# A pre-norm transformer layer on one core: more DMA transposes, zero tiles ahead of the first projection, and x of chunk 1 loaded ahead of the v weights

## The chip, the cores and the metric

One core of a Trainium2 chip runs the whole layer. The metric is the device time of one execution in microseconds (us); lower is better. Each time is printed beside the span of the trace (first to last instruction), and the time was the span plus 1.7 to 2.0 us, mostly 1.8, in every run of this case. In the profile's lines PE is TensorE (matrix products), DVE is VectorE, ACT is ScalarE, POOL is GpSimd and SP is SyncE, which issues most DMA transfers. The granted clock is the share of its full clock that TensorE was given; a stretch below it is called cold here. A zero tile is a matrix product of zeros whose result nobody uses.

Every set of runs was taken with runs of the kernel before on the same chip. A ratio compares a kernel's fast runs with the fast runs of the kernel before in the same rounds. It is therefore not quite the ratio of the medians quoted beside it. Below 1 is faster. Runs marked slow are left out of ratios.

## The reference, cut to what matters

```python
x = A_x                                            # 1 x 2048 x 512, bf16
h  = x + attention(layernorm(x), wqkv) @ wo        # 32 heads of 16; each position looks at
                                                   # 8 keys, 2 apart, itself and backwards
h2 = h + (relu_gate(layernorm(h) @ W_gate) * (layernorm(h) @ W_up)) @ W_down   # F = 1376
```

## The kernel before

The 2048 rows go in four chunks of 512, and a chunk in four blocks of 128 rows. Per chunk: layer norm, transposes, q/k/v projections on TensorE; products q times shifted k on VectorE (`pr`, 128x4096, 2.3 us each), sums over a head on TensorE; products of weights and v on VectorE (`mu`), whose eight terms are then added up; output projection; second norm; MLP. TensorE's work of one chunk covers the waits of another. The order of every instruction on every engine comes from a list of ranks, `RANK`, worked out beforehand from assumed durations. The parts that matter here:

```python
# setup: loads in the order of their queue
for j in range(BPC):                       # x of chunk 0, four blocks, two issuers
    (nc.scalar if j % 2 else nc.sync).dma_start(x_sm[:, j:j + 1, :], x_rows[:, j:j + 1, :])
for c, q in enumerate((nc.sync, nc.scalar, nc.sync)):          # q, k, v weights
    q.dma_start(w3_sb[c][:], w3_r[:, :, c * D:(c + 1) * D])
for tk in range(1, NCK):                                       # x of chunks 1, 2, 3
    nc.sync.dma_start(x_sm[:, tk * BPC:(tk + 1) * BPC, :], x_rows[:, tk * BPC:(tk + 1) * BPC, :])
# ... (cut: other weights)

# layer norm: a block is transposed by a DMA or on TensorE
if (ln, tk, j0) in DMAT:
    nc.sync.dma_start_transpose(out=dst.t[:, :, j * P:(j + 1) * P], in_=xn.t[:])
# ... else four nc.tensor.transpose and an eviction

# attention: the first of three halvings of the eight v products, 128x2048
if n == 4 and (tk, t) in DACC:
    nc.gpsimd.dma_start(mt.t[:, 0:4, :], mt.t[:, 4:8, :], accum_op=ALU.add)   # an accumulating DMA
# ... else one VectorE add

DACC = tuple((k, t) for k in range(3) for t in range(4))       # chunks 0 to 2, all four
DMAT = (("h",2,0),("h",2,2),("x",3,0),("x",3,2))               # x3 and the second norm of chunk 2
NWARM = 48                                                     # opening zero tiles on TensorE
```

The softmax here doesn't subtract the row's maximum and nothing guards it: scores larger than these inputs give would overflow.

Of the kernel before, what the change touches and what calls it, by code (L numbers as in the profile page):

```python
# [8 lines left out]
P = 128  # L9
# [3 lines left out]
ACT = mybir.ActivationFunctionType  # L13
# [4 lines left out]
RANK = [  # L18
    1, 3, 5, 2, 0, 4, 54, 6, 7, 30, 160, 197, 186, 250, 712, 8, 11, 10, 12, 14,
    17, 23, 27, 32, 20, 26, 31, 16, 18, 21, 24, 28, 33, 37, 9, 13, 15, 19, 22, 25,  # L20
    29, 34, 35, 65, 71, 68, 70, 73, 38, 60, 66, 56, 63, 69, 51, 61, 43, 55, 40, 50,
    45, 58, 83, 145, 79, 154, 76, 162, 74, 99, 80, 86, 96, 104, 110, 75, 67, 85, 89, 90,
    171, 179, 185, 114, 136, 123, 133, 128, 94, 113, 101, 108, 118, 148, 159, 183, 189, 193, 156, 170,
    199, 203, 205, 165, 176, 201, 204, 207, 142, 152, 181, 187, 192, 211, 218, 210, 215, 214, 222, 209,
    212, 227, 234, 221, 225, 228, 232, 226, 231, 239, 241, 246, 256, 249, 257, 261, 244, 259, 251, 260,
    264, 292, 321, 277, 317, 267, 313, 324, 333, 340, 280, 305, 270, 304, 301, 308, 303, 310, 315, 295,
    325, 307, 328, 285, 323, 319, 329, 335, 327, 344, 297, 341, 331, 346, 314, 339, 349, 350, 366, 343,
    358, 338, 365, 355, 372, 392, 334, 359, 348, 362, 397, 401, 421, 691, 717, 393, 407, 694, 718, 357,
    420, 701, 721, 363, 423, 699, 720, 39, 47, 44, 48, 36, 41, 42, 46, 49, 52, 62, 78, 64,
    77, 82, 57, 81, 59, 72, 84, 144, 191, 124, 188, 91, 178, 102, 182, 88, 164, 109, 169, 143,  # L30
    172, 117, 168, 147, 252, 139, 300, 87, 299, 151, 302, 195, 174, 224, 245, 229, 208, 238, 248, 253,
    258, 268, 273, 271, 284, 293, 296, 294, 290, 275, 283, 286, 287, 289, 298, 309, 345, 352, 318, 330,
    361, 367, 326, 337, 364, 368, 306, 316, 347, 351, 373, 378, 379, 386, 376, 382, 383, 395, 385, 389,
    391, 396, 390, 394, 398, 400, 402, 403, 406, 413, 408, 415, 419, 411, 417, 412, 418, 422, 431, 456,
    427, 454, 433, 460, 426, 452, 494, 439, 469, 441, 471, 434, 462, 436, 463, 500, 438, 466, 437, 465,
    479, 488, 464, 474, 503, 487, 496, 484, 491, 489, 498, 493, 501, 507, 450, 518, 458, 517, 506, 523,
    499, 520, 526, 447, 508, 444, 509, 524, 516, 536, 709, 726, 510, 530, 707, 725, 522, 538, 705, 723,
    533, 537, 703, 722, 98, 105, 92, 97, 93, 103, 53, 95, 112, 116, 126, 132, 125, 130, 146, 131,
    137, 129, 135, 150, 167, 216, 177, 217, 184, 220, 194, 223, 161, 240, 157, 237, 163, 242, 153, 213,
    173, 428, 175, 409, 202, 416, 219, 356, 236, 254, 265, 312, 274, 263, 288, 320, 322, 332, 336, 342,  # L40
    360, 353, 377, 375, 369, 374, 371, 384, 387, 381, 380, 430, 435, 453, 459, 414, 429, 446, 449, 424,
    432, 451, 457, 399, 425, 443, 448, 467, 473, 461, 468, 475, 482, 470, 478, 477, 480, 472, 476, 485,
    486, 481, 483, 490, 495, 519, 521, 511, 513, 528, 531, 497, 502, 543, 559, 540, 558, 549, 568, 548,
    565, 573, 560, 585, 567, 582, 575, 588, 544, 561, 594, 556, 578, 583, 593, 554, 576, 579, 590, 596,
    552, 570, 563, 580, 546, 564, 553, 574, 591, 616, 625, 572, 618, 599, 621, 608, 623, 631, 620, 630,
    587, 628, 633, 626, 642, 715, 731, 612, 639, 713, 729, 597, 635, 711, 727, 600, 640, 714, 730, 100,
    106, 115, 121, 111, 119, 107, 120, 122, 127, 140, 149, 155, 166, 134, 141, 138, 158, 247, 281, 180,
    255, 196, 269, 190, 266, 243, 279, 235, 278, 200, 272, 230, 276, 233, 541, 198, 505, 262, 550, 206,
    545, 291, 282, 311, 404, 370, 354, 388, 405, 410, 440, 442, 492, 445, 504, 529, 534, 527, 532, 455,
    525, 514, 515, 512, 542, 562, 581, 586, 535, 539, 555, 569, 551, 557, 566, 571, 547, 577, 584, 589,  # L50
    595, 603, 604, 611, 598, 607, 592, 601, 606, 609, 614, 615, 610, 613, 602, 605, 617, 619, 622, 624,
    636, 637, 641, 627, 634, 629, 632, 638, 646, 660, 650, 663, 647, 661, 644, 656, 675, 667, 677, 665,
    674, 673, 681, 670, 678, 684, 659, 671, 654, 668, 657, 669, 662, 672, 682, 651, 664, 652, 666, 643,
    655, 645, 658, 679, 683, 695, 648, 686, 680, 693, 649, 689, 697, 653, 688, 676, 690, 696, 685, 706,
    728, 736, 692, 700, 716, 732, 687, 702, 719, 734, 698, 704, 724, 735, 708, 710, 733, 737,
# [36 lines left out]
class Plan:  # L92
# [21 lines left out]
    GUIDE = ()  # L114

    def order(self):
        for kx, cx, ky, cy in self.GUIDE:
            xs = [o for o in self.ops if o.key and o.key[0].startswith(kx) and o.key[1] == cx]
            for o in self.ops:
                if o.key and o.key[0].startswith(ky) and o.key[1] == cy:  # L120
                    o.deps += xs
        waiting = list(self.ops)
        free = {}
        while waiting:
            best = {}
            for op in waiting:
# [33 lines left out]
            t, op = pick  # L160
# [11 lines left out]
            waiting.remove(op)  # L172
# [4 lines left out]
def kernel(  # L177
# [88 lines left out]
    def setup():  # L266
# [4 lines left out]
        for c, q in enumerate((nc.sync, nc.scalar, nc.sync)):  # L271
            q.dma_start(w3_sb[c][:], w3_r[:, :, c * D:(c + 1) * D])
        for tk in range(1, NCK):
            nc.sync.dma_start(x_sm[:, tk * BPC:(tk + 1) * BPC, :], x_rows[:, tk * BPC:(tk + 1) * BPC, :])

        nc.sync.dma_start(wo_sb[:], A_wo.rearrange("(p t) f -> p t f", t=NT))
        nc.sync.dma_start(wu_sb[:], B_W_up.rearrange("(dt p) f -> p dt f", p=P))
        nc.sync.dma_start(wg_sb[:], B_W_gate.rearrange("(dt p) f -> p dt f", p=P))
        nc.sync.dma_start(
            wd_sb[:, 0:NFF, :], B_W_down[0:NFF * P, :].rearrange("(ft p) n -> p ft n", p=P))  # L280
        if FTAIL:
            nc.sync.dma_start(wd_sb[:FTAIL, NFF, :], B_W_down[NFF * P:F, :])

# [10 lines left out]
        nc.gpsimd.memset(vT[:, :, 0:PADL], 0.0)  # L294

# [20 lines left out]
    DACC = tuple((k, t) for k in range(3) for t in range(4))  # L316
    DAL = 5.5
    TDD, TDL = 2.4, 1.6
    NWARM = 48
    DMAT = (("h",2,0),("h",2,2),("x",3,0),("x",3,2))  # L320
# [8 lines left out]

    LNA = ((0, 0, 0, 0), (0, 0, 0, 0))  # L330
# [5 lines left out]
    A5, A10, AX, AS = 0.52, 0.92, 0.8, 0.2  # L336
# [4 lines left out]
    def load(t):  # L341
        return add(None, "LD", 0.0, None, lat=t)

    xload = [[load(t) for t in (3.4, 3.5, 3.9, 3.9)]] + [[load(t)] * BPC for t in (9.7, 11.2, 12.7)]
    wload = {n: load(t) for n, t in
             (("q", 6.3), ("k", 7.0), ("v", 8.3), ("o", 14.0), ("u", 18.0), ("g", 22.0), ("d", 27.0))}

# [493 lines left out]
```

## Time and profile before

| | before |
|---|---|
| time, median of 3 | 203.58 us |
| the profiled execution | 205.38 us, span 203.6, mean granted clock 0.983 |
| first projection | 10.13 us, on the q weights |
| VectorE's first product q times k | 18.84 us |
| TensorE's last result is evicted from | 200.69 us |

These are the waits of TensorE in the kernel before (who waited for whom: total us, times, longest). The first two lie ahead of the first projection (the 0.8 at 6.68, before the transposes); after it there are only 0.4 us.

```profile
PE bank L511 <- DMA wq_sb<-in_A_wqkv_dram: 2.1, 1, 2.1
PE bank L465 <- DVE row L436: 0.8, 1, 0.8
PE bank L511 <- issue: 0.4, 2, 0.2
```

VectorE in order of time (start, duration, line, tiles; the bracket is the idle time before). It sits idle for 4.94 us until x of chunk 1 has landed, does the statistics of chunk 1 and of half of chunk 2 and the normalisation of chunk 1, and only then the first product of chunk 0.

```profile
13.20 1.29 DVE L401 BATCH_NORM_STATS2 st<-x_sm 128x6 f32<-128x512 bf16 x2 [4.94 <-DMA x_sm<-in_A_x_dram]
...
18.84 2.29 DVE L558 TENSOR_TENSOR big<-quad,kT 128x4096 bf16<-128x4096 bf16 x1
```

One line, the last of the view of the eight DMA transposes:

```profile
DMA to landing us min/median/max: 2.4/2.5/5.4
```

### The profile page before, as it was taken

The numbers are of one execution on the slowest core, as the hardware profiler recorded it, in microseconds if no ns is written. First come the engines' busy times: TensorE is split into PE (matmuls) and PEld (weight loads), VectorE is DVE, ScalarE is ACT, GpSimd is POOL, SyncE is SP. The second block draws the span as 40 slices with busy tenths as digits, with TensorE's granted clock in tenths as the row PEclk, the third lists the DMA queues.
The fourth block names the chain that finished last, engine by engine and source line by source line (L and its number), as shares of the span: only waits on it lengthen the run. The fifth ranks groups of instructions, "written<-read, shape, count | busy, mean of one in ns | idle before, by whom it ended". The sixth has DMA issues, their size and how long they took to land.

```text
span 203.6 us, 2957 instructions
## 1 busy us (share of the span) xinstructions
PE 195.4 (96%) x1102; PEld 96.8 (48%) x1123; DVE 155.1 (76%) x246; ACT 127.7 (63%) x253; POOL 12.6 (6%) x26
## 2 busy tenths in 40 slices
PE   8499999999999999999999999999999999999994
PEld 8347545555545334444454444444444445444452
DVE  6549999999999999999999966599996255021314
ACT  3517879986569993797756599703665353576400
POOL 3000000330000002400033000000000000000000
PEclk9859999999999999999999999999999999999999
DMA  5999901698000002980059900400011001100003
GB/s 187 350 379 403 322 19 30 123 203 163 3 0 0 0 3 52 192 168 0 3 103 180 209 31 0 90 13 0 3 41 62 0 0 53 53 0 0 0 3 103
DMA packets 14893, 18.04 MB, mean 89 GB/s; under 512 B 5056, under 2 KB 12192, under 8 KB 14880
## 3 DMA queue, kind: packets, MB, share of 16 engines
q1 hardware_dynamic: 12336, 10.78, 16.4%
q0 software_dynamic: 1728, 6.29, 16.3%
q10 hardware_dynamic: 816, 0.79, 1.1%
q8 instruction: 9, 0.15, 0.3%
q14 instruction: 4, 0.03, 0.0%
HBM read 8.42 MB, written 2.10 MB: 52 GB/s over the span
## 4 chain that ended last, share of the span: by engine, by line
PE 93%; DMA 4%; issue 1%; SPq 0%; DVE 0%
PE bank L736 38%; PE bank L511 22%; PE bank L773 19%; PE bank L698 7%; DMA wq_sb<-in_A_wqkv_dram 4%; PE bank L564 4%; PE bank L465 2%; PE bank L625 1%; PE bank L597 1%; SPq L270 0%; DVE row L784 0%
## 5 line engine op out<-in xcount | busy, mean ns | idle before, releaser
L736 PE MATMUL bank<-quad,wg_sb 128*128 128x512 bf16 (+1 forms) x171 | 42.3, 379 | 0.3
L736 PE MATMUL bank<-quad,wu_sb 128*128 128x512 bf16 (+1 forms) x173 | 42.3, 379 | 0.1
L743 ACT ACTIVATE gr<-bank 128x512 bf16<-128x512 f32 (+1 forms) x44 | 26.0, 604 | 23.7 <-PE bank L736 18.3
L773 PE MATMUL bank<-wd_sb,gT 128*128 128x512 bf16 (+3 forms) x184 | 39.7, 366 | 0.2
L558 DVE TENSOR_TENSOR big<-quad,kT 128x4096 bf16<-128x4096 bf16 x16 | 36.0, 2284 | 0.1
L646 DVE TENSOR_TENSOR big<-big,vT 128x4096 bf16<-128x4096 bf16 x16 | 35.8, 2283 | 0.3 <-ACT big L631 0.3
L740 ACT CAST up_sb<-bank 128x512 bf16<-128x512 f32 (+1 forms) x44 | 25.7, 594 | 12.3 <-PE bank L736 8.5
L756 DVE TENSOR_TENSOR gT<-gr,up_sb 128x1024 bf16<-128x1024 bf16 (+1 forms) x24 | 15.4, 643 | 20.4 <-ACT gr L743 14.1
L773 PEld LDWEIGHTS <-gT 128*128 128x128 bf16 (+1 forms) x187 | 18.0, 98 | 19.3 <-issue 0.4
L736 PEld LDWEIGHTS <-wu_sb 128*128 128x128 bf16 (+1 forms) x176 | 17.3, 100 | 20.7 <-issue 1.3
L736 PEld LDWEIGHTS <-wg_sb 128*128 128x128 bf16 (+1 forms) x176 | 17.3, 100 | 20.6 <-issue 1.1
L511 PE MATMUL bank<-quad,wq_sb 128*128 128x512 bf16 (+1 forms) x70 | 16.9, 382 | 2.5 <-DMA wq_sb<-in_A_wqkv_dram 2.1
L631 ACT CAST big<-bank 128x512 bf16<-128x512 f32 x32 | 17.2, 610 | 1.5 <-PE bank L625 1.3
L511 PE MATMUL bank<-quad,wk_sb 128*128 128x512 bf16 (+1 forms) x70 | 16.8, 373 | 0.1
L678 POOL DMA_DIRECT2D big<-big x12 | 10.7, 894 | 98.3 <-DVE big L646 95.2
L784 DVE TENSOR_TENSOR row<-x_sm,bank 128x512 bf16<-128x512 bf16 (+1 forms) x17 | 10.6, 652 | 7.8 <-PE bank L773 7.8
L649 DVE TENSOR_TENSOR big<-big 128x1024 bf16<-128x1024 bf16 (+2 forms) x24 | 16.4, 727 | 0.0
L709 DVE SCALAR_TENSOR_TENSOR x_sm<-x_sm,bank 128x512 bf16<-128x512 bf16 x16 | 10.9, 685 | 6.8 <-PE bank L698 6.7
L511 PE MATMUL bank<-quad,wv_sb 128*128 128x512 bf16 x62 | 15.4, 379 | 0.1
L698 PE MATMUL bank<-wo_sb,quad 128*128 128x512 bf16 x61 | 14.8, 379 | 0.2
L371 ACT ACTIVATE row<-x_sm,mv 128x512 bf16<-128x512 bf16 x16 | 11.5, 717 | 4.5 <-DVE mv L363 4.4
L519 ACT CAST quad<-bank 128x512 bf16<-128x512 f32 x16 | 9.6, 601 | 7.4 <-PE bank L511 7.4
(65 smaller groups left out, 161.7 us busy)
## 6 DMA issues: line engine op xcount, KB each, us to landing
big<-big POOLq DMA_DIRECT2D x12, 512.0 KB, 5.5
out_dram<-row SPq DMA_DIRECT2D x15, 128.0 KB, 1.7
x_sm<-in_A_x_dram SPq DMA_DIRECT2D x3, 512.0 KB, 11.0
wu_sb<-in_B_W_up_dram SPq DMA_DIRECT2D x1, 1376.0 KB, 10.6
wg_sb<-in_B_W_gate_dram SPq DMA_DIRECT2D x1, 1376.0 KB, 13.9
wd_sb<-in_B_W_down_dram SPq DMA_DIRECT2D x1, 1280.0 KB, 15.7
wq_sb<-in_A_wqkv_dram SPq DMA_DIRECT2D x1, 512.0 KB, 8.4
wk_sb<-in_A_wqkv_dram ACTq DMA_DIRECT2D x1, 512.0 KB, 8.6
```

The costliest lines, as they stand in the source:

```text
L371: nc.scalar.activation(out=xn.t[:], in_=h.t[:] if h else x_sm[:, tk * BPC + j, :], func=ACT.Square, bias=mv.t[:, j, 0:1], scale=1.0, accum ...
L511: nc.tensor.matmul(mm.t[:, lo:hi], lhsT=w3_sb[c][:, dt, t:D:NT], rhs=xnT.t[:, dt, lo:hi], start=(dt == 0), stop=(dt == NT - 1))
L558: V.tensor_tensor(out=pb.t[:].rearrange("p (t w) s -> p t w s", t=2), in0=q4, in1=k4, op=ALU.mult)
L631: nc.scalar.copy(out=ab.t[:, w, :], in_=bc.t[:])
L646: V.tensor_tensor(out=mt.t[:], in0=ab.t[:], in1=v8, op=ALU.mult)
L649: V.tensor_tensor(out=mt.t[:, 0:n, :], in0=mt.t[:, 0:n, :], in1=mt.t[:, n:2 * n, :], op=ALU.add)
L698: nc.tensor.matmul(od.t[:], lhsT=OT.t[:, t, j * P:(j + 1) * P], rhs=wo_sb[:, t, :], start=(t == 0), stop=(t == NT - 1 and tk not in RPE))
L736: nc.tensor.matmul(mm.t[:fs, :], lhsT=w_sb[:, dt, ft * P: ft * P + fs], rhs=hnT.t[:, dt, :], start=(dt == 0), stop=(dt == NT - 1))
L740: nc.scalar.copy(out=ub.t[:fs, i, :], in_=um.t[:fs, :])
L743: nc.scalar.activation(out=gr.t[:fs, i, :], in_=gm.t[:fs, :], func=ACT.Relu)
L756: V.tensor_tensor(out=gt.t[:fs, 0:n, :], in0=gr.t[:fs, 0:n, :], in1=ub.t[:fs, 0:n, :], op=ALU.mult)
L773: nc.tensor.matmul(od.t[:, c0:c1], lhsT=gts[ft].t[:fs, ft % 2, j * P:(j + 1) * P], rhs=wd_sb[:fs, ft, c0:c1], start=(ft == 0), stop=(ft == ...
```

## The change

Its intent: take 32 transposes off TensorE and give them to DMAs that do not run beside accumulating DMAs; keep TensorE fed with zero tiles until the first projection, so that its clock stays up; get q, k and x of chunk 1 in sooner. The core of the diff (cut: all of `RANK`, planned durations, and moving `f_warm`):

```diff
-        for c, q in enumerate((nc.sync, nc.scalar, nc.sync)):
-            q.dma_start(w3_sb[c][:], w3_r[:, :, c * D:(c + 1) * D])
-        for tk in range(1, NCK):
-            nc.sync.dma_start(x_sm[:, tk * BPC:(tk + 1) * BPC, :], x_rows[:, tk * BPC:(tk + 1) * BPC, :])
+        for dt, q in ((0, nc.sync), (2, nc.scalar)):                 # q in halves, two issuers
+            q.dma_start(w3_sb[0][:, dt:dt + 2, :], w3_r[:, dt:dt + 2, 0:D])
 ...
+        nc.gpsimd.tensor_copy(out=w3_sb[1][0:1, 0, 0:1], in_=x_sm[0:1, 0, 0:1])   # holds k back
+        for c, tk in ((1, 1), (2, 2)):                               # k, x1, v, x2
+            nc.sync.dma_start(w3_sb[c][:], w3_r[:, :, c * D:(c + 1) * D])
+            nc.sync.dma_start(x_sm[:, tk * BPC:(tk + 1) * BPC, :], x_rows[:, tk * BPC:(tk + 1) * BPC, :])
 ...
-    DACC = tuple((k, t) for k in range(3) for t in range(4))
+    DACC = tuple((k, t) for k in range(3) for t in range(4) if k or t < 2)
-    NWARM = 48
-    DMAT = (("h",2,0),("h",2,2),("x",3,0),("x",3,2))
+    NWARM, NFILL = 48, 9
+    DMAT = (('h',2,0),('h',2,2),('x',3,0),('x',3,2),('h',1,0),('h',1,2),('x',2,0),('x',2,2))
+    HG = ([[0, 1], [2, 3]], [[0, 1, 2, 3]], [[0, 1, 2, 3]], [[0, 1, 2, 3]])
+    GUIDE = (("xre0", 0, "xsq", 0), ("xtd", 2, "ta", 0), ("xtd", 3, "ta", 0), ("htd", 1, "ta", 2))
 ...
                     ds.append(add((ln + "tp" + gk, tk), "PE", 4 * TP, f_tp, [a], ...))
+                    if tk == 0 and not residual:
+                        fill(ds[-1])                                 # nine zero tiles
```

`GUIDE` only tells the planner that the transposes of x2 and x3 (`xtd`) come before the accumulating DMAs of chunk 0 (`ta`). It changes planned times and so the order on each engine; it puts no wait into the program.

## The prediction

> **What bounds the kernel now.** I read the page's table of engines first, then the 40 slices, the chain that ended last, the waits of TensorE, and last the opening 26 us in windows of one microsecond.
>
> ```profile
> PE 195.4 (96%) x1102; PEld 96.8 (48%) x1123; DVE 155.1 (76%) x246; ACT 127.7 (63%) x253; POOL 12.6 (6%) x26
> ...
> DVE  6549999999999999999999966599996255021314
> ...
> PEclk9859999999999999999999999999999999999999
> ...
> PE 93%; DMA 4%; issue 1%; SPq 0%; DVE 0%
> ```
>
> TensorE is busy 96% of 203.6 us and carries 93% of the chain. The only other thing on the chain is a DMA, 4%. VectorE is full from slice 3 to slice 22 and has room later. So time can come from three places only: less work on TensorE, an earlier start of its real work, and a faster clock, which is low in slices 1 and 2 alone. The chain in order of time shows the start and the end:
>
> ```profile
> 1.66 8.42 DMA wq_sb<-in_A_wqkv_dram
> 10.08 0.05 issue
> 10.13 2.32 PE bank L511 x9
> ...
> 33.31 0.89 PE bank L465 x16
> ...
> 142.98 10.74 PE bank L736 x49
> ...
> 194.39 6.27 PE bank L773 x39
> 200.66 0.02 issue
> ```
>
> The first projection starts at 10.13, when the q weights land; from there TensorE is on the chain without a real wait until 200.66, and 2.9 us of eviction and output transfer follow. Two unit prices come from here: sixteen 128x128 transposes take 0.89, so 0.056 each, and 128x512 matmuls follow each other every 0.2155 (10.74 over 50, one record missing). The windows of the start (PE, weight loads, DVE, ACT, POOL, granted clock, DMA share, GB/s):
>
> ```profile
> 7.00:8.00 1.00, 1.00 (x14) 0.68 (x12) 1.00 (x4) 0.56 (x1) 0.00 (x0) 1.00 1.11 350
> 8.00:9.00 1.00, 0.05 (x1) 0.00 (x0) 0.26 (x1) 0.61 (x2) 0.00 (x0) 0.90 0.96 310
> 9.00:10.00 1.00, 0.00 (x0) 0.00 (x0) 0.00 (x0) 0.00 (x0) 0.00 (x0) 0.50 1.09 382
> 10.00:11.00 1.00, 0.87 (x5) 0.62 (x6) 0.00 (x0) 0.00 (x0) 0.00 (x0) 0.50 1.10 367
> 15.00:16.00 1.00, 1.00 (x5) 0.38 (x3) 1.00 (x6) 0.53 (x1) 0.00 (x0) 0.69 1.05 402
> 16.00:17.00 1.00, 1.00 (x7) 0.51 (x5) 1.00 (x2) 0.56 (x3) 0.00 (x0) 1.00 1.01 392
> ```
>
> TensorE stands still from 8.05 to 10.13; the clock falls to a half at about 8.8 and comes back at about 15.6. So 5.5 us of projections run at half speed: 2.75 us lost, plus the 2.1 us of standing. The start is where the money is.
>
> **What the Trainium skill says.** "TensorE: Matmul & The Clock Gate", Part 1 (The HAM clock gate): the array's clock is halved after about one idle window of 3.4 us and released after one busy window of that length; start to start is 107 ns cold and 56 ns warm for 128 columns, 427 and 216 for 512. The trace agrees: the 48 opening zero tiles take 4.93 us, 103 ns each, although the granted clock is written as 1.00 there; weight loads in the slow stretch start 0.43 apart; and the slow stretch is 6.8 us, two windows. "DMA: Bandwidth & Descriptors", section "Issuing engines are not separate DMA queues": transfers from several issuers share the same 16 DMA engines and interleave. The trace agrees: the 512 KB of q weights took 8.4 us at 310 to 380 GB/s in total, so most of what moved was something else (k and v weights, x of chunk 1). The same page, "Rules for kernel authors", has it that a DMA transpose next to ordinary DMAs needs nothing; accordingly the program order shows no added semaphore between transposes and accumulating DMAs. They are kept apart only by where they stand. No transpose met an accumulation closely in the trace before; the median transpose landed after 2.5 us, the accumulating DMAs after 5.5.
>
> **The change part by part.**
>
> Transposes. 24 row blocks go through TensorE before, 16 after (chunks 0 and 1 of the first norm, 0 and 3 of the second). 8 blocks x 4 transposes x 0.056 = 1.8 us off TensorE, and four ACT evictions of 1.02 us, which are off the path. They become eight DMA transposes issued by SP, about 1.2 us of issue each, landing after 2.5; the MLP and projections that read them stand many matmuls later, so I count nothing for them.
>
> Zero tiles. Four groups of 9. In TensorE's new order two groups (18) stand right after the first two blocks' transposes, one after the other two blocks' transposes and one q half, and one strays to behind the second score group, some 20 us in. The first two groups fill idle time; the other two cost 18 x 0.056 = 1.0 us on the full engine.
>
> Loads. q weights now go in two halves on two issuers, and k, x1, v, x2 wait behind a one-element GpSimd copy that needs x block 0 (landed at 3.48). So q should land by 5.5 to 6.5. But TensorE's new order begins with two halves of **k**, and blocks 2 and 3 are transposed behind them, so the k weights become the start signal. Their estimate: issue at about 3.8, data after 5.1; 1.57 MB must have moved (x of chunk 0, q, k), which the windows before had reached at 6.9. The landing lags the bytes: before, q and k landed at 10.1 and 10.3 although 1.57 MB were through at 6.9, because what was queued behind them interleaved. After, x1 and v are behind k as well, with less queued ahead of it. Between 7.4 and 10.1; I choose 8.1.
>
> First norm. Exp of the first group now precedes the Square of block 3 (0.7 us) on ACT, so its normalisation can start at about 5.5 in place of 6.21 and transposes follow the 48 opening tiles (end 5.92) without a gap. With the zero tiles TensorE is then busy until about 7.6, which leaves about 0.5 us of waiting; the clock should stay up.
>
> VectorE gains two 128x2048 adds (1.23 each) in chunk 0, since two of its four accumulating DMAs go; and statistics of x2 stand before the first products. Before, VectorE ran without a gap from the first product at 18.84 to the end of chunk 0's attention at 53.1. After, I count the first product at 15.5 to 16 and, with 2.3 us of adds and some reordering, the end at 52 to 52.5; TensorE reaches the output projection of chunk 0 at about 52.5. That is tight, and I give it 0.3 us.
>
> The sum. Before: 792 matmuls of 512 columns x 0.2155 = 170.7, 8 score groups x 0.98 = 7.8, 8 broadcasts x 0.33 = 2.6, 80 transposes after the start 4.5: 185.6. With the start at 10.13 and 2.75 lost to the clock, 198.5; the end is at 200.66, so 2.2 of small issue gaps are carried along. After: 170.7 + 7.8 + 2.6 + 56 transposes after the start 3.1 + 18 zero tiles 1.0 = 185.2. Start 8.1, small gaps 2.2, waiting for the eviction of blocks 2 and 3 0.3, for VectorE 0.3: TensorE ends at 196.1; with the tail of 2.9, 199.0. I take 198.9. The gain of 4.7 is 2.75 of clock, 2.0 of earlier start, 0.4 of net work, less 0.6 of new waits. The earlier x1 is in it only through VectorE: it was idle for 4.9 us before 13.2, which cost TensorE nothing then, but which it must give up if TensorE is to start earlier.
>
> **The rivals.** One: the wait moves from q to k. If k lands as late as q did (10.1), TensorE waits from 7.6 to 10, the clock may fall again, and what is left is 0.4 of net work, perhaps with 2.75 of clock: 200.5 to 203. For it speaks that k stands first and is issued two microseconds later than before; against it, that only half as much is queued ahead of it. Two: VectorE becomes the bound in the first hundred microseconds, where it is full already and is given 2.3 us more. Then TensorE's earlier start is spent waiting at the output projection of chunk 0: 200 to 201.5. Against it: it too starts some 3 us earlier, because x1 comes earlier. Three: the DMA transposes land late behind weights or accumulations, and projections of chunk 2 or the MLP of chunk 1 wait: 1 to 3 us more; there are many independent matmuls in between. Four, the good one: k lands by 7.5 and nothing waits: 197.5.
>
> **Range and chances.** 198.9 if the clock holds and k lands near 8. The range 197.2 to 201.6 holds the good case and most of rivals one and two. The 2% line is 199.5; my middle case is only 0.6 us below it, and the rivals all lie above: 62% faster by over 2%, 36% within, 2% slower.
>
> **What would show it.** The granted clock should be 1.00 in every window from 6 to 20 us; the first projection matmul should read the k weights at 7.5 to 8.5; TensorE should have no wait over 0.5 us afterwards; its busy time without zero tiles should fall by about 1.8 us; DMA transposes should land in about 2.5. Wrong would be: clock 0.50 anywhere after 8 us, a TensorE wait on k of over 1.5 us, or waits of TensorE on VectorE summing to over 1 us.

## The result, and the profile after

The changed kernel took 206.57 us (median of 4, 205.99 to 207.43) against 203.56 us in the same rounds: ratio 1.0148, interval 1.0106 to 1.0191. That is slower by 1.5%, inside the band "within 2%", and far outside the predicted range of 197.2 to 201.6. Neither the number nor its direction was right.

The page of the changed kernel. The clock is full in every slice. TensorE's busy time is 194.3 us against 195.4, but the two can't be compared: the 195.4 holds the cold stretch, and a warm repeat of the kernel before has 192.9; the pages of before and its repeat lack 21 records of matrix products each, this one 19. But the chain that ended last is no longer TensorE's: VectorE now holds 36% of it.

```profile
PE 194.3 (95%) x1108; PEld 97.4 (47%) x1127; DVE 156.1 (76%) x248; ACT 121.2 (59%) x251; POOL 10.8 (5%) x25
...
PEclk9999999999999999999999999999999999999999
...
PE 43%; DVE 36%; DMA 8%; issue 5%; ACT 5%; SPq 1%; POOL 0%; DVEq 0%
```

The waits of TensorE in the changed kernel, in the same columns as before. L541 is a projection, L594 the sum over a head, L766 the MLP. New is a wait of 1.7 us for a DMA transpose (`quad<-row`).

```profile
PE bank L541 <- DMA quad<-row: 1.7, 1, 1.7
...
PE bank L594 <- DVE big L588: 0.9, 1, 0.9
PE bank L541 <- DMA wk_sb<-in_A_wqkv_dram: 0.6, 1, 0.6
PE bank L766 <- ACT quad L516: 0.6, 1, 0.6
```

The chain of waits of the changed kernel, in order of time (start, duration, what). Read it from above: x of chunk 2, the fourth load in the queue, lands at 14.34, VectorE does its statistics, and its products run one after the other from 16.85; then the last DMA transpose of x3, issued at 38.92, lands only 4.71 us later. TensorE, which needs it for chunk 3's k, projects that and then chunk 2's v; ScalarE evicts this v and behind it, in its order, chunk 2's k, which TensorE had projected before 41.3; and VectorE starts its next product, of chunk 1, at 46.80 after 1.8 us of standing still.

```profile
5.26 9.08 DMA x_sm<-in_A_x_dram
...
16.93 4.40 DVE big L588 x2
...
37.10 1.82 DVE big L676
38.92 4.71 DMA quad<-row
43.63 0.14 issue
43.76 1.91 PE bank L541 x8
...
45.69 0.59 ACT vT L549
46.27 0.50 ACT kT L549
...
46.80 2.29 DVE big L588
```

That last wait is not for data. The product reads chunk 1's columns of `kT`, whose evictions had ended by 42.0. In the program as it is built from the changed kernel, its wait is on the eviction into column 1040 of `kT`, which is chunk 2's (chunk 1 ends at 1039). The experiments below never took this wait away by itself.

The windows of the changed kernel (columns as in the prediction). In 8 to 9 TensorE still waits for k, but at full clock. In 40 to 50 TensorE loses 1.7 us and VectorE 1.8; in 60 to 70 TensorE loses 0.9 while VectorE and ACT are full.

```profile
8.00:9.00 1.00, 0.36 (x7) 0.19 (x5) 0.60 (x2) 0.00 (x0) 0.00 (x0) 1.00 0.97 335
...
40.00:50.00 10.00, 8.33 (x39) 4.21 (x38) 8.18 (x9) 5.28 (x10) 0.86 (x1) 1.00 0.60 110
60.00:70.00 10.00, 9.09 (x68) 4.36 (x68) 9.96 (x16) 9.85 (x24) 0.00 (x0) 1.00 0.00 0
```

The end has grown too: from the start of TensorE's last eviction to the end of the span it is 205.6 - 200.86 = 4.7 us, and 203.6 - 200.69 = 2.9 before. The packed traces divide it: until the last store has landed 2.8 us (2.0 before), and from there to the end 1.9 (0.9 before).

Of the prediction's own signs the full clock came true. Against it stand TensorE's waits of 1.7, 0.9 and 0.6 us, its waits for VectorE of 1.1 in sum after the opening (0.9 in the lines above), and two DMA transposes of sixteen that landed after 5.7 and 4.7 us in place of 2.5.

### The profile page after: what moved, and what is told of

It is laid out like the page before. It is cut to its first block, busy times and chain, and to the rows that moved or that the text cites. A ratio compares the mean times of both kernels' runs of the same rounds, so it can differ in the third digit from the quotient of the medians.

```text
span 205.6 us, 2952 instructions
## 1 busy us (share of the span) xinstructions
PE 194.3 (95%) x1108; PEld 97.4 (47%) x1127; DVE 156.1 (76%) x248; ACT 121.2 (59%) x251; POOL 10.8 (5%) x25
## 4 chain that ended last, share of the span: by engine, by line
PE 43%; DVE 36%; DMA 8%; issue 5%; ACT 5%; SPq 1%; POOL 0%; DVEq 0%
PE bank L766 24%; PE bank L803 14%; DVE big L588 12%; DVE big L676 10%; DMA x_sm<-in_A_x_dram 6%; PE bank L728 3%; DVE big L679 2%; DVE row L471 2%; DMA quad<-row 2%; DVE x_sm L739 2%; DVE st L436 2%; DVE gT L786 2%; DVE row L814 1%; PE bank L541 1%; ACT quad L516 1%
## 5 line engine op out<-in xcount | busy, mean ns | idle before, releaser
L766 PE MATMUL bank<-quad,wu_sb 128*128 128x512 bf16 (+1 forms) x175 | 42.4, 379 | 0.2
L766 PE MATMUL bank<-quad,wg_sb 128*128 128x512 bf16 (+1 forms) x170 | 41.4, 379 | 0.9 <-ACT quad L516 0.6
L770 ACT CAST up_sb<-bank 128x512 bf16<-128x512 f32 (+1 forms) x44 | 25.1, 591 | 21.1 <-PE bank L766 20.3
L766 PEld LDWEIGHTS <-wg_sb 128*128 128x128 bf16 (+1 forms) x176 | 17.5, 100 | 21.2 <-issue 1.3
L766 PEld LDWEIGHTS <-wu_sb 128*128 128x128 bf16 (+1 forms) x176 | 17.4, 100 | 20.9 <-issue 1.0
L679 DVE TENSOR_TENSOR big<-big 128x1024 bf16<-128x1024 bf16 (+2 forms) x26 | 18.9, 768 | 0.0
L541 PE MATMUL bank<-quad,wk_sb 128*128 128x512 bf16 (+1 forms) x71 | 16.3, 356 | 2.4 <-DMA quad<-row 1.7
L541 PE MATMUL bank<-quad,wq_sb 128*128 128x512 bf16 (+1 forms) x69 | 16.0, 355 | 0.1
L541 PE MATMUL bank<-quad,wv_sb 128*128 128x512 bf16 x62 | 15.9, 379 | 0.2
L708 POOL DMA_DIRECT2D big<-big x10 | 8.8, 877 | 100.9 <-DVE big L676 65.4
L471 DVE TENSOR_SCALAR row<-x_sm,mv,rs 128x512 bf16<-128x512 bf16 x32 | 11.7, 405 | 2.7 <-ACT rs L453 2.6
L406 ACT ACTIVATE row<-x_sm,mv 128x512 bf16<-128x512 bf16 x16 | 11.4, 717 | 3.7 <-DVE mv L398 3.6
```

The source lines that it names most:

```text
L471: V.tensor_scalar(out=xn.t[:], in0=x, scalar1=mv.t[:, j, 0:1], scalar2=rs.t[:, j:j + 1], op0=ALU.add if residual else ALU.subtract, op1=AL ...
L541: nc.tensor.matmul(mm.t[:, lo:hi], lhsT=w3_sb[c][:, dt, t:D:NT], rhs=xnT.t[:, dt, lo:hi], start=(dt == 0), stop=(dt == NT - 1))
L679: V.tensor_tensor(out=mt.t[:, 0:n, :], in0=mt.t[:, 0:n, :], in1=mt.t[:, n:2 * n, :], op=ALU.add)
L766: nc.tensor.matmul(mm.t[:fs, :], lhsT=w_sb[:, dt, ft * P: ft * P + fs], rhs=hnT.t[:, dt, :], start=(dt == 0), stop=(dt == NT - 1))
L770: nc.scalar.copy(out=ub.t[:fs, i, :], in_=um.t[:fs, :])
```

## The experiments

Three theories stood after the first look.

- A: the start is worth what the prediction said, and the changed kernel gives it back in new waits (transposes, stores).
- B: the start is worth little, because VectorE and the landing of x of chunks 1 and 2 bound the first sixty microseconds whatever TensorE does.
- C: the two added VectorE additions are what costs.

Kernels named "before plus a part" have the order of before on each engine with that part put in; kernels "of the changed one" have the order of the changed kernel. `RANK` was renumbered for each, which is not shown. The first three groups ran beside kernels before at 203.99, 203.95 and 203.88 us (medians of 11).

### The kernel before again

No edit.

> The kernel before, unchanged, to have the span and the granted clock of each timed execution, which the first job gave for the changed kernel only. The profiled execution of before took 205.4 us where the timed ones took 203.6, and ran with the clock at half for 6.8 us. Theory A (the clock's window falls differently from execution to execution): the timed executions show a mean clock above the 0.983 of that profile and spans of 201.5 to 202.5, so before loses less to the clock than I took from its profile. Theory B (profiling alone costs 1.8 us): mean clock 0.983 in all of them.

Measured: 204.24 us, ratio 0.9997 (0.9974 to 1.0021). This time the profiled execution had a clock of 0.999 and its first projection at 9.91, and still took 204.24. Its last result was evicted at 199.60, 1.1 us sooner than in the cold profile (200.69), not 2.75. Of the first line below 1.5 us lie ahead of the first projection; 0.7 of it and the 0.5 of the last are waits for VectorE after it, which the cold profile did not have:

```profile
PE bank L465 <- DVE row L436: 2.2, 2, 1.5
PE bank L511 <- DMA wq_sb<-in_A_wqkv_dram: 1.7, 1, 1.7
...
PE bank L564 <- DVE big L558: 0.5, 1, 0.5
```

So the kernel before has a warm clock in most of its executions. All 61 timed ones together (these six and the 55 beside the other groups) say what the clock is worth in it: 36 with a clock of 0.997 and above took 203.72 us in the mean, 23 with 0.989 to 0.992 took 204.10, and two with 0.983 took 205.34 and 205.70 (the last marked slow). The middle group was 0.3 to 0.5 us slower on each of the three chips. The timed runs of this group had clocks of 0.989 to 1.00, so the timed median never held the 2.75 us. Against A.

### The new loads alone

The setup and load order of the change (first part of the diff above) in the kernel before.

> Before, in before's order of instructions, with the changed kernel's order of loads alone (q in halves on two issuers; k, x1, v, x2 behind the one-element copy). If an earlier start of TensorE is worth its length: q lands by 6.5, the first projection starts at about 8.3 in place of 10.1, and the time falls by 1.5 to 3 us. If VectorE bounds the first 100 us: TensorE starts earlier, then waits at the scores or the output projection of chunk 0, and the time falls by the earlier start of VectorE's first product only (0 to 1.5 us).

Measured: 203.24 us, ratio 0.9976 (0.994 to 1.0013). In its profile x of chunk 1 is used from 10.72 in place of 13.20 and the first product starts at 16.18. Against 4.75 us that the prediction had for start and clock, this is 0.5, and not distinguished from nothing. One of its runs had a clock of 0.99 and took 205.41, the others 202.67 to 203.8.

### The zero tiles alone

`NFILL = 9` and `fill(...)` in the kernel before, its loads untouched.

> Before, with 36 zero tiles put between the transposes of chunk 0 and the first projection, loads as before. Clock theory: the granted clock stays at 1.00 after 8 us and, against executions with the full cold stretch, 2.75 us are gained; against the timed executions of before the gain is what they lose to the clock, 1 to 2.8 us. If the cold stretch is an accident of the profiled execution, the gain is under 0.5 us.

Measured: 203.99 us, ratio 0.9999 (0.9968 to 1.0031). The clock in its profile still fell to 0.50 between 10 and 12: the first group of tiles needs the first transposes, and TensorE was idle for most of the time from 6 to 8, ahead of them. All 36 tiles then ran in one row from 9.05 on, and the first projection came behind them at 12.61, not at 10.1. So this run does not test the clock by itself. It tests something else: TensorE started 2.7 us later than in the warm repeat (9.9), at a full clock from 12.3, and its last result came only 0.9 us later (200.46 against 199.60). For B.

### The changed kernel with its last stores in the order of VectorE

```diff
-  SP issues the last stores from row buffers 108, 110, 109, 107, 111
+  SP issues the last stores from row buffers 107, 108, 109, 110, 111   (VectorE's order)
```

> The changed kernel with the last five output stores issued in the order in which VectorE finishes them; nothing else differs. In its trace the store of the first finished block stands behind three others, and the last store is issued at 202.1 although VectorE is done at 201.3 (before: 201.1 and 201.1). Tail theory: 0.7 to 1.7 us less than the changed kernel, about 205. Rival (the stores are held by the DMA queues, whatever their order): no difference over 0.3 us.

Measured: 205.83 us, ratio 1.0094 (1.0075 to 1.0114). These are the last output stores on SP's queue (start, duration), of the kernel before, of the changed one and of this one:

```profile
201.13 0.33 SPq L788 DMA_DIRECT2D out_dram<-row  x1
```

```profile
201.56 0.92 SPq L818 DMA_DIRECT2D out_dram<-row  x2
```

```profile
200.55 0.37 SPq L818 DMA_DIRECT2D out_dram<-row  x1
```

In the changed kernel two stores are still to be issued after VectorE has finished (201.28), because the store of buffer 110, VectorE's fourth, stands second in the queue and holds two finished ones behind it. Put in order, that is worth 1.0148 - 1.0094, or 1.1 us; the traces have 0.8, from the start of the last eviction to the landing of the last store (2.83 and 2.02). From last eviction to end it is then 3.9 us, here and in the further repair below, against 2.9 before. The packed traces show where the rest lies: behind the landing of the last store, where SyncE passes the final waits of the program one by one. In the kernel before one such wait was left when the last store landed, and 0.9 us to the end; here eight were left, and 1.85 us. The last store's own wait stands second in that row here and last before.

### The transposes alone

```diff
-    DMAT = (("h",2,0),("h",2,2),("x",3,0),("x",3,2))
+    DMAT = (('h',2,0),('h',2,2),('x',3,0),('x',3,2),('h',1,0),('h',1,2),('x',2,0),('x',2,2))
```

This in the order of the kernel before, so nothing keeps the transposes away from accumulating DMAs.

> Before with the transposes of x2 and h1 by DMA, and nothing else of the change: loads, accumulating DMAs (four in chunk 0) and the order of the rest stay. If TensorE's work is the bound: 1.8 us less. If the eight transposes of x2 and x3 in a row on SP (1.25 to 1.3 us each, 10 us) run into the four accumulating DMAs of chunk 0: the last of x3 lands after 45 us, TensorE waits for it by 2 us or more in its own order, VectorE then waits for k of chunk 1, and the time rises by 1 to 3 us.

Measured: 221.82 us, ratio 1.0867 (1.0816 to 1.0918). The chain of waits, TensorE's waits and the window show it. SP issues the transposes of the second norm of chunk 1 from 104.3 to 113.0, beside four accumulating DMAs issued by GpSimd at 104.23, 107.73, 109.93 and 112.38; the transpose issued at 109.96 landed 10.57 us later.

```profile
109.96 10.57 DMA quad<-row
```

```profile
PE bank L747 <- DMA quad<-row: 13.4, 1, 13.4
```

```profile
100.00:150.00 50.00, 36.60 (x174) 15.77 (x167) 29.65 (x52) 24.23 (x53) 3.71 (x4) 0.86 0.45 74
```

TensorE stands for 13.4 us and its clock falls on top (0.86 in this stretch). The expectation had the cost in chunk 0, at x3's transposes; there TensorE waited 2.6 us, and the larger part came here. Placed badly, the same transposes that save 1.8 us of TensorE cost 18. So the planner's idea of keeping them clear was needed; the question is whether it was reached.

### Two more VectorE additions alone

```diff
-    DACC = tuple((k, t) for k in range(3) for t in range(4))
+    DACC = tuple((k, t) for k in range(3) for t in range(4) if k or t < 2)
```

This in the kernel before.

> Before with two of chunk 0's four accumulating DMAs replaced by two 128x2048 adds on VectorE (1.15 us apart each), nothing else. If VectorE bounds the kernel up to the attention of chunk 2: the time rises by 1.5 to 2.5 us. If TensorE alone bounds it: under 0.5 us, and less if the accumulating DMAs were waited for.

Measured: 205.81 us, ratio 1.0094 (1.005 to 1.0138): two additions of 1.23 us cost 1.9. TensorE then waits 1.1 us for VectorE at the output projection of chunk 0, and was busy 8.94 of the 10 us from 50 on, against 9.95 before. In the order of before, VectorE's work in the first sixty microseconds reaches the end almost whole. For B and, so far, for C.

### x2 back on TensorE

The stores in order, and in `DMAT` the two entries of x2 taken out again.

> The changed kernel, stores in order as in the last run, with the four blocks of x2 transposed by TensorE again (0.9 us of TensorE, two evictions); x3, h1 and h2 stay with the DMA. Collision theory (eight transposes in a row on SP bring the last of x3 behind the first accumulating DMA): with four in a row the last of x3 is issued as soon as VectorE has it, lands before 41 us, the waits of TensorE and of VectorE in 40 to 50 us go, and the time falls by 1 to 2 us against the 205.8 of the run with stores in order, in spite of 0.9 us more TensorE work. Rival (the loss is VectorE's two adds and its own idle time elsewhere): within 0.5 us of 205.8 or above.

Measured: 205.27 us, ratio 1.0061 (1.003 to 1.0091). The collision is not gone: x3's last transpose was issued at 37.77, 0.6 us after the first accumulation (37.16), and landed after 5.0 us, at 42.8; the expectation had it land before 41. Only the wait for it is gone. TensorE's order, with x2's transposes and evictions in it, gains a new wait on ACT of 0.9, and VectorE still waits 1.2 us for an eviction into `kT`. Nor does its gain of 0.7 us come from there: from the first product to the last eviction it takes 184.15 us, against 183.97 with the stores alone, while from the last store's landing to the end it takes 1.08 against 1.85. So this run neither shows the collision nor speaks against it.

### The accumulation later

The stores in order, and two of VectorE's v products of chunk 0 exchanged:

```diff
-  VectorE: v product of tile 0 (its accumulating DMA follows) ... v product of tile 2
+  VectorE: v product of tile 2 (added up by VectorE) ... v product of tile 0
```

> The changed kernel, stores in order, with one exchange on VectorE: the product with v of tile 2 (tree on VectorE) goes before the one of tile 0 (tree by accumulating DMA), so that the first accumulating DMA starts 2.2 us later, at 39.5, after the last transpose of x3 has been issued at 38.9. If the accumulating DMA is what made that transpose take 4.7 us in place of 2.5: it lands by 41.5 to 42, the 1.6 us wait of TensorE and the 1.8 us of VectorE fall to under 0.6 each, and the time falls by 1 to 2 us against 205.8. If the transpose is slow for another reason (the queue of eight): no change there.

Measured: 204.32 us, ratio 1.0016 (0.9985 to 1.0046), 1.5 us faster than with the stores alone. The first line below is the first accumulating DMA of the changed kernel, the second that of this one; the last of the eight transposes was issued at 38.92 in the changed kernel, after the accumulation, and took 2.7 us to issue; here all eight are issued in 10.47 us in place of 11.96, and the last, issued 0.7 us ahead of the accumulation, lands after 2.4.

```profile
37.36 1.01 POOL L708 DMA_DIRECT2D big<-big  x1 [33.65 <-DVE row L471]
```

```profile
38.84 1.01 POOL L708 DMA_DIRECT2D big<-big  x1 [35.13 <-DVE big L676]
```

The wait for DMA transposes is gone, and TensorE and VectorE are both full from 40 to 50 (10.00 and 10.00). In the changed kernel the last transpose was issued 1.56 us after the accumulation; against the run with the stores alone the exchange moved the accumulation by 2.2 us (36.66 to 38.84). From first product to last eviction it takes 1.8 us less (table below). Stores and collision, 1.1 and 1.5 us, are 2.6 of the 3.0 us by which the changed kernel is slower. And without both it is no better than before.

### The changed kernel again

No edit.

> The changed kernel, unchanged, so that its time stands beside the others of one job. Ratio to before 1.010 to 1.019 as in the first job (about 206.5 us). The same two waits of TensorE as before: 1.5 to 1.8 us for a DMA transpose in 40 to 45 us, 0.6 us for an eviction of chunk 0's second norm near 65 us.

Measured: 207.17 us, ratio 1.0163 (1.0133 to 1.0193). The result and its waits repeat: 1.7 us for a transpose, 0.9 for k, 0.6 for ACT, 0.6 for VectorE.

### The two additions left out

The repaired kernel above with the two 128x2048 additions of chunk 0 missing. Its result is wrong (relative error 0.25); it shows what the two additions cost there.

```diff
             for n, du in ((4, D20), (2, D10), (1, D2)):
+                if n == 4 and tk == 0 and t > 1:
+                    continue
```

> WRONG RESULT ON PURPOSE: the kernel of the run with the accumulation later (stores in order, first accumulating DMA after x3's transposes), with the two 128x2048 adds of chunk 0 that the change put on VectorE simply left out, neither on VectorE nor by DMA. It measures what these adds cost inside the changed kernel. If VectorE is the bound there: 1.5 to 2.3 us less than that run (ratio to before about 0.992). If TensorE bounds it: under 0.5 us.

Measured: 204.43 us, ratio 1.0036 (1.0011 to 1.0061): nothing gained against 1.0016. VectorE is busy 8.21 of the 10 us from 50 on and TensorE all 10. Against C in the changed kernel, though it held in the order of before: the two orders are bounded differently. (The profiled execution waited 2.2 us for k and had its first product late, at 17.17; from there to its last eviction it took 182.15 us, against 182.17 with the additions.)

### No zero tiles in the repaired kernel

```diff
-                    if tk == 0 and not residual:
-                        fill(ds[-1])
```

> The kernel of the run with the accumulation later, without the four groups of zero tiles. If the zero tiles hold the clock up: the granted clock falls to 0.5 for 3 to 7 us after 8 us in some executions, and the time rises or is the same. If they only fill TensorE (18 of the 36 stand on a full engine, 1.0 us): the clock stays above 0.99 as in the run with the loads alone, and the time falls by 0 to 1 us. VectorE-bound theory: under 0.5 us either way.

Measured: 206.77 us, ratio 1.0133 (1.0088 to 1.0179). Its profiled execution was a slow one (208.15), but five of six runs had a clock of 0.983 to 0.992, the sixth 1.00 at 204.98. The windows show what the tiles hold off: TensorE idle, then the clock halved.

```profile
8.00:10.00 2.00, 0.00 (x0) 0.00 (x0) 0.60 (x2) 0.00 (x0) 0.00 (x0) 0.75 0.99 308
10.00:12.00 2.00, 1.73 (x9) 1.22 (x10) 0.00 (x0) 0.00 (x0) 0.00 (x0) 0.50 1.02 342
```

In the repaired kernel, where TensorE waits for k, the tiles are worth about 2.4 us. Placed as they were in the kernel before, they were worth nothing.

### A first attempt at something better

The repaired kernel without zero tiles, with the q projections ahead of the k projections, and two of the statistics of x2 behind the first products.

> The same without zero tiles, with TensorE beginning with the q halves (q lands at 6.5, k at 8.9) and with two of the statistics of x2 moved behind the first products on VectorE. If VectorE bounds the first half: the first product starts up to 1.3 us earlier (about 15), limited by the evictions of q and k; the time falls by 0.5 to 1.5 us against the run without zero tiles and lands near or under before (ratio 0.990 to 1.000).

Measured: 206.13 us, ratio 1.0071 (1.0027 to 1.0115), two of six runs slow. The first product came at 16.12, no earlier, and TensorE gained waits on VectorE of 1.3, 1.3 and 1.1 us. It took back about half of what the missing tiles cost (1.0133 to 1.0071), as expected of it, but did not come near the kernel before. The rest is a miss: the first product did not move.

### q first in the repaired kernel

The order of the first projections as in before, both q halves first, everything else as in the repaired kernel, zero tiles included. Beside it and the next one the kernel before took 203.95 us.

> This is e8 with the first projections of chunk 0 put back into the order of before: both q halves, then blocks 2 and 3, then both k halves; zero tiles, loads, adds and transposes stay. If the k weights as start signal cost the changed kernel what the prediction's term says (first projection at 8.95 where q has landed by 6.5), TensorE's first projection falls to about 7.6 to 8.3, no wait on k is over 0.5 us, and the time falls by 0.6 to 1.2 us against e8: ratio to before 0.994 to 0.999. If the first half is bounded by VectorE and the landing of x of chunk 1, an earlier first projection only lengthens TensorE's waits on VectorE before 30 us: ratio stays 1.000 to 1.003.

Measured: 204.24 us, ratio 1.0018 (0.999 to 1.0047), the same as the repaired kernel. TensorE's first projection is at 7.9 in place of 8.8, nothing waits for k, the clock is 1.00 in all six runs; and TensorE waits 1.1 us for VectorE's product instead. For B: that k became the start signal cost nothing.

### The new loads with a longer opening

The kernel before with the new loads, and `NWARM = 58` in place of 48.

> This is e2 (before with the loads of after) with 58 opening zero tiles in place of 48: ten more at 0.056 to 0.1 us lie in the time in which TensorE waits for the first transposes. If part of e2's timed executions lost the clock for a window, they go now: all runs at clock 1.00, ratio to before 0.992 to 0.997 and no run over 204.5. If the clock was not on the path in e2 either, ratio stays at 0.996 to 0.999; if the ten tiles push the first transposes back, 0.998 to 1.001.

Measured: 203.02 us, ratio 0.9951 (0.9932 to 0.997), six runs from 202.42 to 203.59 with the clock at 0.998 to 1.00. The ten tiles close the gap in which the loads-only kernel lost the clock in some runs, and half a per cent is the first gain that the interval keeps.

### x of chunk 1 behind the v weights again

The kernel just told, with one line's order changed: k, v, x1, x2. The last three ran together; the kernel before took 204.10 us there and spread more than usual (202.05 to 205.7), so they are best compared with one another.

> This is e14 with x of chunk 1 put back behind the v weights (k, v, x1, x2), everything else as in e14; the first projection, on q, stays at 8.1. In the five fast profiles of the order of before, the span less the start of VectorE's first product was 184.3 to 184.8. If the landing of x1 sets the end through VectorE's first product, x1 lands about 13, the first product starts near 18, the span is the product's start plus 184.5, and the ratio to before goes from 0.995 to 0.999 to 1.002 although TensorE starts 1.8 us earlier than in before. If the start of TensorE's projections or its clock sets the end, the ratio stays at 0.994 to 0.997.

Measured: 203.75 us, ratio 1.0026 (0.9976 to 1.0077); four runs at clock 1.00 from 203.50 to 203.80, two at 0.992 at 205.2 and 205.39. x1 is used from 12.03, not much later than 11.43 in its base, and the first product starts at 17.16. The amount was overrated (18 expected); the relation held, as the table below shows. The chains say why it is so little: in the base it runs through x of chunk 2, which lands at 14.38 and whose first statistics stand ahead of the first product; here x2 lands at 13.51, and the chain runs through x1 (12.01).

### x of chunk 1 ahead of k

```diff
-        nc.gpsimd.tensor_copy(out=w3_sb[1][0:1, 0, 0:1], ...)        # holds k back
-        for c, tk in ((1, 1), (2, 2)):
-            nc.sync.dma_start(w3_sb[c][:], ...)            # k, x1, v, x2
-            nc.sync.dma_start(x_sm[:, tk * BPC:...], ...)
+        nc.gpsimd.tensor_copy(out=x_sm[0:1, BPC, 0:1], ...)          # holds x1 back
+        for c, tk in ((1, 1), (2, 2)):
+            nc.sync.dma_start(x_sm[:, tk * BPC:...], ...)  # x1, k, x2, v
+            nc.sync.dma_start(w3_sb[c][:], ...)
```

> This is e14 with x of chunk 1 ahead of the k weights and x2 ahead of the v weights (x1, k, x2, v). If the landing of x1 and x2 sets the end, the first product starts 1 to 2 us earlier (15 to 15.8) as long as k, which the product needs too, lands by about 10; ratio 0.986 to 0.992. If k, now later, becomes the wait of TensorE or of the first product, or v a later one, the ratio is 0.995 to 1.002.

Measured: 202.13 us, ratio 0.9919 (0.9872 to 0.9965), six runs from 201.55 to 202.67, all at clock 1.00: the fastest kernel, below both. x1 is used from 8.40, x2 lands at 12.88, the first product starts at 15.72, and the bound changes over. Below are the chain's shares in the kernel with the longer opening, then those of this one, and the start of this one's chain: TensorE now runs from the landing of k, 1.6 us after it had asked for it, to the end.

```profile
PE 84%; DVE 7%; DMA 6%; SPq 1%; issue 0%; POOL 0%
```

```profile
PE 93%; DMA 5%; DVE 0%; SPq 0%; issue 0%; POOL 0%
```

```profile
3.96 7.42 DMA wk_sb<-in_A_wqkv_dram
...
11.42 5.40 PE bank L528 x36
```

### The longer opening again

No edit against the kernel two above.

> This is e14 again, for the comparison on the same chip, and to see whether its gain holds: ratio to before 0.993 to 0.998.

Measured: 203.27 us, ratio 0.9988 (0.9941 to 1.0036), one run at 204.76. Its gain over the kernel before is therefore small and not firm: 0.3 us here, 1.0 there. Against it on the same chip, x1 ahead of k is 202.11 / 203.43 = 0.9935 in the means, or 1.3 us.

### What the profiles say together

From each profile: the start of the first projection, of VectorE's first product, of the eviction of TensorE's last result, and the difference of the last two.

| kernel | first projection | first product | last eviction | difference |
|---|---|---|---|---|
| before (cold for two windows) | 10.1 | 18.84 | 200.69 | 181.85 |
| before again (warm) | 9.9 | 18.21 | 199.60 | 181.39 |
| zero tiles alone (cold for one window) | 12.6 | 18.62 | 200.46 | 181.84 |
| new loads alone | 8.1 | 16.18 | 197.57 | 181.39 |
| longer opening | 8.1 | 16.84 | 198.24 | 181.40 |
| longer opening, again | 8.0 | 16.89 | 198.27 | 181.38 |
| x1 behind v | 7.9 | 17.16 | 198.54 | 181.38 |
| x1 ahead of k | 7.9 | 15.72 | 197.57 | 181.85 |
| changed kernel | 9.0 | 16.85 | 200.86 | 184.01 |
| changed kernel again | 8.9 | 16.55 | 200.59 | 184.04 |
| its stores in order | 9.2 | 16.13 | 200.10 | 183.97 |
| repaired | 8.8 | 16.08 | 198.25 | 182.17 |
| repaired, q first | 7.9 | 16.23 | 198.41 | 182.18 |

In five warm profiles with before's order the end is the first product plus 181.38 to 181.40, while the first projection moved from 9.9 to 7.9. That is the bound of the start: VectorE's first product, not TensorE's first projection. Three profiles are 0.46 over the constant: x1 ahead of k, the zero tiles alone and the kernel before in its cold execution. In these three TensorE has 93 to 94% of the chain, in the five others 83 to 84%, so there TensorE did set the end.

## Why the prediction was wrong, by its own steps

1. **The base.** The sum was laid out on the span of the profiled execution (203.6) and its result, 199.0, was written down as a time. Time is span plus 1.8, and the profiled execution had taken 205.38, not 203.58; so 1.8 us of the forecast gain was never there. By its own steps the sum should have read 200.8.

2. **The clock, worth 2.75 us.** This is the step that failed in mechanism. The clock stays at 1.00 in the changed kernel, as predicted. But the kernel before, warm in a profile of its own, ended only 1.1 us sooner, with new waits for VectorE of 1.2; and in its timed executions, most of them warm, a clock of 0.99 cost 0.4 us (204.10 against 203.72). The long cold stretch that the prediction priced was in two of 61. The reading "TensorE is 93% of the chain, so its lost time is the loss" held for one cold execution only; VectorE stood close behind it. Once the loads are ahead, a cold window costs more (205.2 and 205.39 against 203.5 to 203.8 in one kernel), so there the tiles are needed.

3. **The earlier start, worth 2.0 us.** k as start signal landed at 8.9 and not at 8.1, but this does not matter: with the first projection at 7.9 the time was the same. What sets the start is VectorE's first product. It came at 16.85 where 15.5 to 16 was predicted, behind the landing of x of chunk 2 at 14.34, for which the prediction had no figure; and the gain from all of start and clock is 0.3 to 1.0 us in the best form that keeps the change's load order (two measurements of the longer opening).

4. **DMA transposes, counted as nothing.** This step failed, and the rival "land late: 1 to 3 us more" is what happened. The prediction saw that only program order keeps them from the accumulations, and then trusted the planned times. Its reading that no transpose met an accumulation closely in the trace before was wrong: one did, 0.17 us apart, and landed after 5.4 us. In the changed kernel two did (5.7 and 4.7). Moving one accumulation by 2.2 us gave 1.5 us back.

5. **VectorE, allowed 0.3 us of waiting.** The second rival, that VectorE is the bound of the first half, was right, and was priced too low. That its 2.3 us of new additions are the cause was right only for the order of before (1.9 us); in the repaired kernel leaving them out changed nothing. The largest wait of VectorE, 1.8 us, came from the late transpose of step 4.

6. **The tail, carried along at 2.9 us.** It became 4.7, and putting the last stores in order gave back 1.1 us of time. This could have been read from the changed program before any run; the prediction looked at the order of the other engines only. The repaired kernel's tail is still 0.9 to 1.0 us longer than that of before, nearly all of it behind the landing of the last store, in SyncE's final waits. Some 0.4 of it appears with the order of before and the new loads too (1.33 us from landing to end, against 0.90).

7. **TensorE's work, 0.8 us net off.** As a count right (64 transposes in place of 96, 84 zero tiles in place of 48 in the traces); the busy times don't measure it, as said above. It is worth nothing while VectorE and the second norm of chunk 0 hold TensorE up: the repaired kernel has 182.17 in the table against 181.39.

Added up in spans, the miss on the changed kernel's median is 204.8 - 199.0 = 5.8: 2.6 in stores and collision, shown one at a time, and 3.2 in the bound of the start and the rest of the tail, which the repaired kernel shows together (202.5 - 199.0 = 3.5, the difference being spread between sets of runs). With the 1.8 of step 1 it is 7.6 of the 7.7 us. The 3.2 is what is left over and was not taken apart further. Two sums of the prediction are a little off and change nothing: the parts of its gain add to 4.55, not 4.7, and 10.74 over 50 is 0.2148, not 0.2155.

Still open: why the final waits take 0.9 to 1.0 us longer with the changed order (eight are passed after the landing, two of them slowly, where one was before; no run changed it); the wait of 0.6 us for ACT in the second norm of chunk 0, split in two groups by the change; and VectorE's wait for chunk 2's k. None of the three was tried by itself.

## What to carry to other kernels

An engine that has 93% of the chain in one profile may have another one right behind it: before pricing a gain at the start, follow the second engine back to what released its first long instruction, and price the gain from the later of the two. Check that the profiled execution took the time of the timed ones, and keep spans and times apart. Where only program order keeps two kinds of DMA apart, treat the distance as unproven until the trace shows it; read the order of every queue of the changed program, the last stores too; and look up in the program which write a long wait is for, since it need not be the one whose data is read.

## What the Trainium skill lacked or had wrong

- "DMA: Bandwidth & Descriptors", section "Rules for kernel authors": that a transpose next to ordinary DMAs needs nothing held for correctness (every result was right but that of the run that left work out), but not for time. A transpose landed after a median of 2.5 us alone; after 4.7 to 5.7 when issued up to 1.6 us behind one accumulating DMA (5.4 in the kernel before); and after 10.6 among four. One issued 0.7 us ahead of the accumulation landed after 2.4. The issue on SP took 2.7 us in place of 1.2 in the changed kernel's last one. No page read for this gives that cost.
- The same page, section "Issuing engines are not separate DMA queues": agreed. What it gives no figure for is what the place of a load among the others is worth: with the same q loads ahead, x of chunk 1 was used from 12.0 us behind k and v, from 11.4 between them and from 8.4 ahead of both, and the last cost the k weights 1.6 us of TensorE's waiting.
- "TensorE: Matmul & The Clock Gate", Part 1: its spacings agreed (103 ns cold, 56 warm), and so did its word that the cold stretch differs from run to run: executions of one and the same program had clocks of 1.00, 0.99 or 0.983 in the mean. So the cold stretch of a single profile is not the cold stretch of the timed runs. What a cold stretch costs in a kernel with a second engine close behind no page read for this says: here 0.4 us for 0.99 and 1.6 and more for 0.983 (205.34 us and above against 203.72).
